# A norm's product and low half on GpSimd instead of VectorE, for fifteen of sixteen pairs of heads

## The chip, the cores and the metric

One core of a Trainium2 chip runs the whole kernel; the other cores do nothing. The metric is the device time of one launch in microseconds (us). The engines are named as in the profile: PE is TensorE (matmuls), PEld its weight loads, DVE is VectorE, ACT is ScalarE, POOL is GpSimd, and SP is the engine whose queue issues most of the DMA transfers. Each engine works through its own instructions in the order in which the program gives them, and waits on semaphores for what the others must have finished.

## The reference

The block computes a layer norm of `x` (2048 rows of 576), an attention with 32 heads of 18, a gated linear unit of width 4608, and joins them:

```
xn = layernorm(x)
q, k, v = heads(xn @ wqkv)                     # 32 heads of 18
p = softmax(q @ k.T * 18 ** -0.5)
s = merge_heads(p @ v) @ wo
h = gelu(xn @ w_gate) * (xn @ w_up)
out = x + s * silu(h @ w_down)
```

The division of the softmax is what this case is about: `p @ v` is summed with unnormalized weights, and each head's sum is multiplied afterwards by the reciprocal of the sum of its weights.

## The kernel before

The products that need precision are done with pairs of 16-bit numbers: a value is split into a high half (the value rounded to 16 bits) and a low half (the value minus the high half), and three matmuls replace one.

Attention goes over 16 pairs of heads. For a pair, the query positions are handled in two halves of 1024 (`qh`), the key positions in 16 tiles. The loop at the end of the program runs over 64 blocks for each pair. A block gives PE one product of keys and queries (`qk2`, L1342), whose exponential ACT takes (L1348, or L1350 and L1351 where the two heads have different scales), and one product for the row maxima of the next pair (`qk1`, L1290), of which DVE takes the maximum (L1293). Each of these two results lives in one double bank of PSUM, so the next block's product waits until ACT, or DVE, has read the last one. The rest of a block's PE time is filled with matmuls of the gated linear unit: gate and up products (L473), down products (L733), and every few blocks a burst of `p @ v` products (L1367), which DVE adds up in a tile `osb` of 128 by 512 (L1375, or L1373 for the first). In the last pair the gate and up products are at an end, and the output products with `wo` (L912) take their place.

POOL carries the gelu of the gated unit: four instructions after ACT has copied the gate product `gs` out of PSUM (L661 to L664), then, when ACT has taken a tanh (L667), two more (L674, L675), and, when ACT has rounded the high half `hhi` (L689), the low half `hlo` (L696). It also makes the low halves of the weights of the next chunks (L342, L343).

When the last burst of a half of a pair is added up, `norm` begins a chain of small steps, each planned some blocks after the one before. Their names in the code are: `a1` and `a2`, two DMA transfers that fetch the sums of weights; `b`, a reciprocal on DVE; `b1` and `b2`, two transfers that spread the reciprocals over the tile `obr`; `c`, the product of `osb` and `obr` (L1421, on DVE); `d`, the high half `onh` (L1425, on ACT); `e`, the low half `onl` as `osb` minus `onh` (L1429, on DVE); `f`, the stores of both halves to DRAM on SP's queue (L1439). There are 30 such chains, two for each of the first 15 pairs. The last pair has another path (`turn`, `divide`, `back`, then the same `d` and `e`).

What order all this has is fixed when the program is written out. `Deferred` holds the steps with a due block and a cost. A step on DVE or ACT is let in when the block has room left on that engine (by a table of costs and rooms), a step on POOL when an estimate of POOL's backlog is at most 1.2. The estimate grows by the cost of each POOL step and shrinks by each block's estimated time. The gelu's steps add to it but are not held back by it. The preparation of weights is a queue of its own, `bg`, that takes what room is left in the same block. So a step that costs DVE nothing leaves its room to `bg`, and a step that costs POOL something holds `bg`'s POOL pieces back.

Of the kernel before, what the change touches and what calls it, by code (L numbers as in the profile page):

```python
# [16 lines left out]
ALU = mybir.AluOpType  # L17
# [64 lines left out]
def on_act(t=0.7):  # L82
    return {"A": t}


def on_dve(t=0.7):
    return {"V": t}


def on_pool(t):  # L90
    return {"G": t}
# [3 lines left out]
def kernel(ctx: ExitStack, tc: tile.TileContext, x, wqkv, wo, w_gate, w_up, w_down, out):  # L95
    nc = tc.nc
# [1260 lines left out]
    def burst(todo, tag):  # L1357

        p, qh, k0, _, _ = todo[0]
        k1 = todo[-1][2]  # L1360
        t = MTile(tag, [P, 512], F32, 1)
        for _, _, kt, pa, pb in todo:
            for b, pt in enumerate((pa, pb)):
                for h in range(2):
                    qd = 64 * b + 32 * h
                    c0 = 38 * kt + 19 * h
                    nc.tensor.matmul(  # L1367
                        t.t[qd:qd + 32, :], VT[p][:, c0:c0 + 32], pt[:, h],
                        start=kt == k0, stop=kt == k1, skip_group_check=True,
                    )  # L1370
        if k0 == 0:
            osum[p, qh] = ap.tile([P, 512], F32, tag="osb", name=f"osb_{p}_{qh}", bufs=2)
            nc.vector.tensor_copy(osum[p, qh], t.t)  # L1373
        else:
            nc.vector.tensor_tensor(osum[p, qh], t.t, osum[p, qh], op=ALU.add)  # L1375
        t.done()
        if k1 == NT - 1:
            norm(p, qh)

    def norm(p, qh):  # L1380
        st = {}
        last = p == NPAIR - 1


        def a():
            st["o"] = osum.pop((p, qh))

        def turn():
            st["b"] = ap.tile([P, 512], F32, tag="obr", name=f"obr_{p}_{qh}", bufs=1)
            nc.vector.transpose(st["b"], st["o"])  # L1390

        def divide():
            b = st["b"].rearrange("p (c i) -> p c i", i=32)
            rc = sm.tile([P, 16], F32, tag="oc", name=f"rc_{p}_{qh}", bufs=2)
            nc.vector.reciprocal(rc, b[:, :, DH])
            nc.vector.tensor_tensor(b, b, rc[:, :, None].to_broadcast([P, 16, 32]), op=ALU.mult)

        def back():
            nc.vector.transpose(st["o"], st["b"])

        def a1():
            st["sd"] = dp.tile([4, 512], F32, tag="sd", name=f"sd_{p}_{qh}", bufs=2)
            nc.sync.dma_start(st["sd"], st["o"][18:128:32, :])

        def a2():
            st["c"] = sm.tile([P, 16], F32, tag="oc", name=f"oc_{p}_{qh}", bufs=2)
            nc.sync.dma_start(st["c"], st["sd"].rearrange("a (b c) -> (a b) c", c=16))

        def b():
            nc.vector.reciprocal(st["c"], st["c"])  # L1410

        def b1():
            st["rd"] = dp.tile([4, 512], F32, tag="rd", name=f"rd_{p}_{qh}", bufs=2)
            nc.sync.dma_start(st["rd"].rearrange("a (b c) -> (a b) c", c=16), st["c"])

        def b2():
            st["b"] = ap.tile([P, 512], F32, tag="obr", name=f"obr_{p}_{qh}", bufs=1)
            nc.sync.dma_start(st["b"], st["rd"][:, None, :].to_broadcast([4, 32, 512]))

        def c():  # L1420
            nc.vector.tensor_tensor(st["o"], st["o"], st["b"], op=ALU.mult)  # L1421

        def d():
            st["h"] = wp.tile([P, 512], F16, tag="evh", name=f"onh_{p}_{qh}", bufs=3)
            nc.scalar.activation(st["h"], st["o"], AF.Copy)  # L1425

        def e():
            st["l"] = wp.tile([P, 512], F16, tag="evl", name=f"onl_{p}_{qh}", bufs=3)
            nc.vector.tensor_tensor(st["l"], st["o"], st["h"], op=ALU.subtract)  # L1429

        def f():
            for qb in range(2):
                cols = slice(1024 * qh + 512 * qb, 1024 * qh + 512 * qb + 512)
                for h in range(2):
                    r = DH * (2 * p + h)
                    qd = 64 * qb + 32 * h
                    for key, rows in (("h", oh_rows), ("l", ol_rows)):
                        for r1, i, n in rows(r, DH):
                            nc.sync.dma_start(OHL[r1:r1 + n, cols], st[key][qd + i:qd + i + n, :])  # L1439
            obdone[qh] += 1  # L1440

        def g():
            last_o[qh] = (st["h"], st["l"])

        def chained(*steps):

            (dt, fn, cost), rest = steps[0], steps[1:]

            def run():
                fn()  # L1450
                if rest:
                    chained(*rest)

            defer.at(defer.now + dt, run, cost)

        a()
        if last:
            final_norm.extend([turn, divide, back, d, e, g])
        else:
            dma = ((1, a1, None), (3, a2, None), (3, b, None), (1, b1, None), (2, b2, None))  # L1460
            chained(*dma, (4, c, on_dve()), (1, d, on_act()), (1, e, on_dve()), (1, f, None))

    ctx.enter_context(tc.manual_schedule())
    filler[0] = unit_v(preps[0])
# [160 lines left out]
    for p in range(NPAIR):  # L1625
# [3 lines left out]
        for i in range(4 * NT):  # L1629
# [24 lines left out]
            if gs.left == 0 and gs.pair is None and not gs.closed and not plan:  # L1654
# [3 lines left out]
                d = dn is not None or (  # L1658
                    len(dnq) > 1 and not (more and 57 < i < 61) and held < 5 and (u is None or not u.wide)
                )  # L1660
# [33 lines left out]
            else:  # L1694
# [4 lines left out]
                if step is None:  # L1699
                    d = dn is not None or len(dnq) > 1 and not 58 <= i <= 60 and held < 6  # L1700
                else:
                    d = step[0]
# [103 lines left out]
```

## Time and profile before

| | |
|---|---|
| median of 3 runs | 2588.85 us (2588.57 to 2589.61) |
| the profiled execution's own time | 2589.88 us |
| its span, first to last instruction | 2588.1 us |
| mean granted PE clock | 0.995 |

The profile lists for each engine its busy time, for groups of equal instructions the busy time, the mean of one, and the idle time of their engine just ahead of them with what ended it. A wait of PE is what costs time here if it isn't covered; a wait of the other engines is often only the sign that they had nothing to do.

### The profile page before, as it was taken

The numbers are of one execution on the slowest core, as the hardware profiler recorded it, in microseconds if no ns is written. First come the engines' busy times: TensorE is split into PE (matmuls) and PEld (weight loads), VectorE is DVE, ScalarE is ACT, GpSimd is POOL, SyncE is SP. The second block draws the span as 40 slices with busy tenths as digits, with TensorE's granted clock in tenths as the row PEclk, the third lists the DMA queues.
The fourth block names the chain that finished last, engine by engine and source line by source line (L and its number), as shares of the span: only waits on it lengthen the run. The fifth ranks groups of instructions, "written<-read, shape, count | busy, mean of one in ns | idle before, by whom it ended". The sixth has DMA issues, their size and how long they took to land.

```text
span 2588.1 us, 60831 instructions
## 1 busy us (share of the span) xinstructions
PE 2503.7 (97%) x25800; PEld 1317.9 (51%) x25800; DVE 1898.9 (73%) x2594; ACT 1661.0 (64%) x2081; POOL 1537.7 (59%) x1564
## 2 busy tenths in 40 slices
PE   6889999999999999999999999999999999999998
PEld 6564545455545545455444444455545444454555
DVE  7587778777777778777777777777777777777644
ACT  5225665666777666767666666767666666766664
POOL 4247663586537553758667575848576676757513
PEclk9999999999999999999999999999999999999999
DMA  4431021201120112102010110101111111110124
GB/s 144 129 104 24 12 58 55 63 18 44 39 86 19 32 32 65 44 24 56 9 50 16 35 52 17 50 15 38 29 34 29 38 29 38 26 32 8 41 63 138
DMA packets 134300, 118.68 MB, mean 46 GB/s; under 512 B 60176, under 2 KB 113064, under 8 KB 134028
## 3 DMA queue, kind: packets, MB, share of 16 engines
q1 hardware_dynamic: 128892, 105.23, 14.9%
q0 software_dynamic: 2432, 6.54, 0.7%
q8 instruction: 201, 3.29, 0.5%
q10 hardware_dynamic: 2704, 3.03, 0.4%
q14 instruction: 71, 0.58, 0.1%
HBM read 84.89 MB, written 29.61 MB: 44 GB/s over the span
## 4 chain that ended last, share of the span: by engine, by line
PE 83%; DVE 6%; ACT 4%; POOL 3%; issue 2%; DMA 1%; ACTq 0%; SPq 0%; DVEq 0%; POOLq 0%
PE mb_t L473 16%; PE ma_t L473 15%; PE md_t L733 15%; PE md_t L1367 10%; PE s L1342 8%; PE s L1290 8%; PE ma_t L1367 6%; DVE PM L1293 2%; ACT P L1348 1%; PE md_t L912 1%; DVE osb L1375 1%; PE mb_t L1367 1%; PE mc_t L492 1%; PE mb_t L912 1%; PE pv_t L492 1%
## 5 line engine op out<-in xcount | busy, mean ns | idle before, releaser
L1293 DVE TENSOR_REDUCE PM<-s 128x2 f32<-128x1024 f32 x1024 | 1251.1, 1224 | 340.4 <-PE s L1290 330.9
L1348 ACT ACTIVATE P<-s,etab 128x1024 f32<-128x1024 f32 x896 | 995.6, 1112 | 605.7 <-PE s L1342 591.4
L473 PE MATMUL ma_t<-XHT,whi_c 64*128 64x512 f16 x1440 | 541.3, 376 | 4.0 <-ACT gs L638 2.4
L473 PE MATMUL mb_t<-XHT,whi_c 64*128 64x512 f16 x1440 | 541.0, 376 | 2.9 <-DVE touch L441 1.2
L473 PE MATMUL ma_t<-XHT,wlo_c 64*128 64x512 f16 x1296 | 486.7, 376 | 0.0
L473 PE MATMUL mb_t<-XHT,wlo_c 64*128 64x512 f16 x1152 | 432.5, 375 | 0.0
L473 PE MATMUL ma_t<-XL,whi_c 64*128 64x512 f16 x1152 | 432.5, 375 | 0.0
L473 PE MATMUL mb_t<-XL,whi_c 64*128 64x512 f16 x1152 | 432.3, 375 | 0.0
L1290 PE MATMUL s<-KT,QT 54*128 54x512 f16 x2048 | 399.0, 378 | 16.7 <-DMA QT<-QD 8.2
L1342 PE MATMUL s<-QT,KT 56*128 56x512 f16 x2048 | 405.3, 379 | 8.4 <-ACT P L1348 4.7
L473 PEld LDWEIGHTS <-whi_c 64*128 64x128 f16 x5184 | 274.1, 94 | 236.9 <-issue 18.0
L733 PE MATMUL md_t<-dhi_c,hhi 64*128 64x288 f16 x2304 | 340.9, 283 | 3.5 <-DVE osb L1375 1.5
L733 PE MATMUL md_t<-dhi_c,hlo 64*128 64x288 f16 x2304 | 340.5, 282 | 0.0
L733 PE MATMUL md_t<-dlo_c,hhi 64*128 64x288 f16 x2304 | 340.0, 282 | 0.0
L733 PEld LDWEIGHTS <-hhi 64*128 64x128 f16 x4608 | 245.2, 94 | 138.1 <-issue 17.6
L674 POOL TENSOR_SCALAR tw<-tw 128x512 f32<-128x512 f32 x144 | 91.0, 632 | 364.0 <-ACT tw L667 363.4
L1367 PE MATMUL md_t<-P,VT 128*32 128x512 f32 x2480 | 290.6, 596 | 0.6 <-ACT P L1348 0.5
L696 POOL TENSOR_TENSOR hlo<-gv,hhi 128x512 f16<-128x512 f32 x144 | 167.6, 1164 | 195.1 <-ACT hhi L689 189.0
L1342 PEld LDWEIGHTS <-KT 56*128 56x128 f16 x2048 | 125.2, 94 | 246.8 <-issue 159.3
L661 POOL TENSOR_TENSOR tw<-gs 128x512 f32<-128x512 f32 x144 | 150.6, 1046 | 127.0 <-ACT gs L638 126.7
L753 DVE SCALAR_TENSOR_TENSOR y<-md_t,c_c,y 128x576 f32<-128x576 f32 x272 | 219.2, 806 | 8.3 <-PE md_t L733 8.2
L473 PEld LDWEIGHTS <-wlo_c 64*128 64x128 f16 x2592 | 138.0, 94 | 122.4
(257 smaller groups left out, 4070.2 us busy)
## 6 DMA issues: line engine op xcount, KB each, us to landing
draw_c<-in_B_w_down SPq DMA_DIRECT2D x18, 576.0 KB
raw_c<-in_B_w_gate SPq DMA_DIRECT2D x18, 512.0 KB
raw_c<-in_B_w_up SPq DMA_DIRECT2D x18, 512.0 KB
obr<-rd SPq DMA_DIRECT2D x30, 256.0 KB
KT<-KD SPq DMA_DIRECT2D x32, 224.0 KB
QT<-QD SPq DMA_DIRECT2D x32, 216.0 KB
VS<-vst POOLq DMA_DIRECT2D x16, 304.0 KB, 3.9
VT<-VS SPq DMA_DIRECT2D x16, 304.0 KB
```

Of the source, the lines that this page charges most:

```text
L473: nc.tensor.matmul(o, lw, xx, start=self.stage == 0 and self.k == 0, stop=self.stage == 1 and self.k == self.slots - 1, skip_group_check=True,
L492: nc.tensor.matmul(o, xx(t), ww[:, t, i, :], start=(k == 0), stop=False)
L661: gp.tensor_tensor(st["t"], st["g"], st["g"], op=ALU.mult)
L674: gp.tensor_scalar(st["t"], st["t"], 1.0, 1.0, op0=ALU.mult, op1=ALU.add)
L696: gp.tensor_tensor(hs.lo[:, ft], st["v"], hs.hi[:, ft], op=ALU.subtract)
L733: nc.tensor.matmul(self.t.t[:, hf, 0:288], a[r, ft, sl], b[r, ft, 288 * hf:288 * hf + 288], start=self.stage == 0 and k == 0, stop=self.st ...
L753: nc.vector.scalar_tensor_tensor(yy, y, w.c, yy, op0=ALU.mult, op1=ALU.add)
L1290: nc.tensor.matmul(s1[:, h], QT[p][r, P * qt:P * qt + P], KT[p][r, 512 * kb:512 * kb + 512], start=True, stop=True)
L1293: nc.vector.tensor_reduce(PM[p][:, :, qt, kb:kb + 1], s1, op=ALU.max, axis=AX.X)
L1342: nc.tensor.matmul(s2[:, h], KT[p][r, P * kt:P * kt + P], QT[p][r, 512 * qb:512 * qb + 512], start=True, stop=True)
L1348: nc.scalar.activation(pt, s2, AF.Exp, scale=ETAB[j0])
L1367: nc.tensor.matmul(t.t[qd:qd + 32, :], VT[p][:, c0:c0 + 32], pt[:, h], start=kt == k0, stop=kt == k1, skip_group_check=True,)
```

## The change

Steps `c` and `e` go from DVE to POOL for the first 15 pairs. Their costs in the planner become POOL costs of 1.1 each, and the due distances of `d` and of `f` grow from one block to two. The last pair's `e` stays on DVE.

```diff
         def c():
-            nc.vector.tensor_tensor(st["o"], st["o"], st["b"], op=ALU.mult)
+            nc.gpsimd.tensor_tensor(st["o"], st["o"], st["b"], op=ALU.mult)
...
         def e():
             st["l"] = wp.tile([P, 512], F16, tag="evl", name=f"onl_{p}_{qh}", bufs=3)
-            nc.vector.tensor_tensor(st["l"], st["o"], st["h"], op=ALU.subtract)
+            (nc.vector if last else nc.gpsimd).tensor_tensor(st["l"], st["o"], st["h"], op=ALU.subtract)
...
             dma = ((1, a1, None), (3, a2, None), (3, b, None), (1, b1, None), (2, b2, None))
-            chained(*dma, (4, c, on_dve()), (1, d, on_act()), (1, e, on_dve()), (1, f, None))
+            chained(*dma, (4, c, on_pool(1.1)), (2, d, on_act()), (1, e, on_pool(1.1)), (2, f, None))
```

Two places show how the instructions stand (pairs and halves are counted from 0). The first is in pair 6, where the chain of the second half of pair 5 (its sum is `osb_1_14475`) reaches `c` and `e`. On DVE, before:

```order
L1375 TENSOR_TENSOR osb_0_15468<-md_t,osb_0_15468 128x512
L1293 TENSOR_REDUCE PM_14859<-s_7_22_15899 128x2
L1421 TENSOR_TENSOR osb_1_14475<-osb_1_14475,obr_1_15787 128x512
L441 COPY touch<-md_t 1x2
L1293 TENSOR_REDUCE PM_14859<-s_7_23_15939 128x2
L753 SCALAR_TENSOR_TENSOR y<-md_t,c_c_13853,y 128x576
```

On DVE with the change, at the same place:

```order
L1375 TENSOR_TENSOR osb_0_15461<-md_t,osb_0_15461 128x512
L1293 TENSOR_REDUCE PM_14859<-s_7_22_15897 128x2
L253 TENSOR_REDUCE m_c_15700<-draw_c_15528 128x1
L441 COPY touch<-md_t 1x2
L1293 TENSOR_REDUCE PM_14859<-s_7_23_15938 128x2
L753 SCALAR_TENSOR_TENSOR y<-md_t,c_c_13891,y 128x576
```

`c` is gone, and a maximum over a chunk's weights (L253, from `bg`) stands where it stood, ahead of the small copy L441 for which PE waits. On POOL at the same place, before:

```order
L675 TENSOR_TENSOR gv_3_0_15664<-gv_3_0_15664,tw_3_0_15698 128x512
L696 TENSOR_TENSOR hlo_3_15847<-gv_3_0_15664,hhi_3_15846 128x512
L661 TENSOR_TENSOR tw_3_1_15904<-gs_3_1_15864 128x512
L662 TENSOR_SCALAR tw_3_1_15904<-tw_3_1_15904 128x512
L663 TENSOR_TENSOR tw_3_1_15904<-tw_3_1_15904,gs_3_1_15864 128x512
L664 TENSOR_TENSOR gv_3_1_15876<-gv_3_1_15876,gs_3_1_15864 128x512
L674 TENSOR_SCALAR tw_3_1_15904<-tw_3_1_15904 128x512
L675 TENSOR_TENSOR gv_3_1_15876<-gv_3_1_15876,tw_3_1_15904 128x512
```

On POOL with the change:

```order
L675 TENSOR_TENSOR gv_3_0_15664<-gv_3_0_15664,tw_3_0_15695 128x512
L696 TENSOR_TENSOR hlo_3_15845<-gv_3_0_15664,hhi_3_15844 128x512
L1421 TENSOR_TENSOR osb_1_14475<-osb_1_14475,obr_1_15785 128x512
L661 TENSOR_TENSOR tw_3_1_15902<-gs_3_1_15862 128x512
L662 TENSOR_SCALAR tw_3_1_15902<-tw_3_1_15902 128x512
L663 TENSOR_TENSOR tw_3_1_15902<-tw_3_1_15902,gs_3_1_15862 128x512
L664 TENSOR_TENSOR gv_3_1_15874<-gv_3_1_15874,gs_3_1_15862 128x512
L1429 TENSOR_TENSOR onl_1_16026<-osb_1_14475,onh_1_15991 128x512
L674 TENSOR_SCALAR tw_3_1_15902<-tw_3_1_15902 128x512
L675 TENSOR_TENSOR gv_3_1_15874<-gv_3_1_15874,tw_3_1_15902 128x512
```

`c` now stands ahead of the gelu's first four steps, and `e` between them and L674. In the whole program the instruction behind `c` or `e` on POOL is L674 in 26 of 60 cases, L661 in 13, L696 in 10, and a weight's L342 in 6.

The second place is in pair 2, where the second half of pair 1 (`osb_1_6027`) is normed while the weights of a chunk are split. On ACT, before:

```order
L1348 ACTIVATE P_0_8_7424<-s_2_0_8_7421,etab_375 128x1024
L1348 ACTIVATE P_1_8_7455<-s_2_1_8_7452,etab_375 128x1024
L1425 ACTIVATE onh_1_7461<-osb_1_6027 128x512
L1348 ACTIVATE P_0_9_7482<-s_2_0_9_7479,etab_375 128x1024
L667 ACTIVATE tw_3_0_7431<-tw_3_0_7431 128x512
```

On ACT with the change:

```order
L1348 ACTIVATE P_0_8_7424<-s_2_0_8_7421,etab_375 128x1024
L1348 ACTIVATE P_1_8_7455<-s_2_1_8_7452,etab_375 128x1024
L1348 ACTIVATE P_0_9_7480<-s_2_0_9_7477,etab_375 128x1024
L1425 ACTIVATE onh_1_7486<-osb_1_6027 128x512
L1348 ACTIVATE P_1_9_7503<-s_2_1_9_7500,etab_375 128x1024
L667 ACTIVATE tw_3_0_7431<-tw_3_0_7431 128x512
```

`d` (L1425) stands one exponential later. On POOL there, before:

```order
L664 TENSOR_TENSOR gv_3_0_7401<-gv_3_0_7401,gs_3_0_7389 128x512
L342 TENSOR_SCALAR draw_c_6191<-draw_c_6191,s_c_6927 128x576
L343 TENSOR_TENSOR dlo_c_7404<-draw_c_6191,dhi_c_7403 128x576
L674 TENSOR_SCALAR tw_3_0_7431<-tw_3_0_7431 128x512
L675 TENSOR_TENSOR gv_3_0_7401<-gv_3_0_7401,tw_3_0_7431 128x512
```

On POOL there, with the change:

```order
L664 TENSOR_TENSOR gv_3_0_7401<-gv_3_0_7401,gs_3_0_7389 128x512
L1429 TENSOR_TENSOR onl_1_7510<-osb_1_6027,onh_1_7486 128x512
L342 TENSOR_SCALAR draw_c_6191<-draw_c_6191,s_c_6927 128x576
L343 TENSOR_TENSOR dlo_c_7404<-draw_c_6191,dhi_c_7403 128x576
L674 TENSOR_SCALAR tw_3_0_7431<-tw_3_0_7431 128x512
L675 TENSOR_TENSOR gv_3_0_7401<-gv_3_0_7401,tw_3_0_7431 128x512
```

`e` has come between L664 and the weights' L342, and it waits for `d`. PE has the same instructions as before, and the same order but for three stretches: some 39 blocks in pairs 2 and 3, 24 blocks in pair 9, and parts of the last pair.

## The prediction

> **What bounds the kernel now.** I read the page first: the busy times and the chain that ended last.
>
> ```profile
> span 2588.1 us, 60831 instructions
> PE 2503.7 (97%) x25800; PEld 1317.9 (51%) x25800; DVE 1898.9 (73%) x2594; ACT 1661.0 (64%) x2081; POOL 1537.7 (59%) x1564
> ...
> PE 83%; DVE 6%; ACT 4%; POOL 3%; issue 2%; DMA 1%; ACTq 0%; SPq 0%; DVEq 0%; POOLq 0%
> ```
>
> PE is busy for 97% of the span and holds 83% of the chain. A busy PE is an upper view (ends of matmuls are modelled), but it says where to look: what DVE loses or POOL gains counts only where PE waits for it. All 30 chains run between 340 and 2480 us, so the second view is the windows, cut there (busy us and instructions of PE, PEld, DVE, ACT, POOL; then granted clock, DMA share, GB/s):
>
> ```profile
> 340.00:2480.00 2140.00, 2110.32 (x21767) 1070.03 (x21763) 1610.62 (x2148) 1446.93 (x1788) 1336.59 (x1326) 1.00 0.14 37
> ```
>
> PE idles 2140.0 - 2110.3 = 29.7 us in that stage. DVE idles 529 us and POOL 803 us. The third view is the waits of PE in the same window (total us, times, longest):
>
> ```profile
> PE ma_t L1367 <- ACT gs L638: 4.3, 9, 1.0
> PE s L1342 <- ACT P L1348: 4.0, 5, 1.6
> PE s L1290 <- DVE PM L1293: 3.5, 6, 1.5
> PE ma_t L473 <- DVE osb L1375: 2.6, 5, 1.0
> PE ma_t L1367 <- DVE evl L524: 1.7, 4, 1.0
> PE md_t L1312 <- DVE osb L1375: 1.6, 2, 0.8
> PE md_t L1312 <- DVE rmc L1306: 1.3, 2, 0.8
> ```
>
> No row names the two moved lines, L1421 and L1429, and POOL is not in them. DVE's five rows here make 10.7 us, ACT's two 8.3. The whole stage offers some 11 us on DVE's side, and ACT's side is already as thin. The fourth view is the groups of instructions in that window (busy us, mean ns, then idle time ahead and what ended it):
>
> ```profile
> L1348 ACT ACTIVATE P<-s,etab 128x1024 f32<-128x1024 f32 x795 | 884.3, 1112 | 543.5 <-PE s L1342 531.1 <-PE s L1290 7.9 <-ACT rms L1314 1.1
> L663 POOL TENSOR_TENSOR tw<-tw,gs 128x512 f32<-128x512 f32 x132 | 168.0, 1273 | 11.1
> L696 POOL TENSOR_TENSOR hlo<-gv,hhi 128x512 f16<-128x512 f32 x133 | 154.9, 1165 | 180.7 <-ACT hhi L689 178.3 <-PE ma_t L473 2.2
> L674 POOL TENSOR_SCALAR tw<-tw 128x512 f32<-128x512 f32 x132 | 83.6, 633 | 342.6 <-ACT tw L667 342.1
> L689 ACT ACTIVATE hhi<-gv 128x512 f16<-128x512 f32 x133 | 82.6, 622 | 6.0 <-POOL gv L675 6.0
> L1421 DVE TENSOR_TENSOR osb<-osb,obr 128x512 f32<-128x512 f32 x30 | 25.8, 860 | 0.6 <-DMA obr<-rd 0.6
> L1429 DVE TENSOR_TENSOR onl<-osb,onh 128x512 f16<-128x512 f32 x30 | 24.1, 802 | 0.1
> L253 DVE TENSOR_REDUCE m_c<-draw_c 128x1 f32<-128x576 f32 x32 | 23.3, 742 | 0.0
> ```
>
> **What the change removes.** DVE loses 25.8 + 24.1 = 49.9 us, 3% of its work in the stage. What that is worth is read where PE waited just behind one of these instructions. One such place, on DVE:
>
> ```profile
> 1143.34 1.22 DVE L1293 TENSOR_REDUCE PM<-s 128x2 f32<-128x1024 f32 x1
> 1144.47 1.11 DVE L1421 TENSOR_TENSOR osb<-osb,obr 128x512 f32<-128x512 f32 x1
> 1145.50 0.14 DVE L441 COPY touch<-md_t 1x2 f32<-1x2 f32 x1
> ```
>
> PE's next instruction there:
>
> ```profile
> 1145.69 0.30 PE L733 MATMUL md_t<-dhi_c,hhi 64*128 64x288 f16 x2 [0.46 <-DVE touch L441]
> ```
>
> The copy L441 had to stand behind `c`, and PE waited 0.46 us for it. I went back from every wait of PE for DVE to see whether `c` or `e` stood in the unbroken run of DVE work ahead of it. There are six such places; these are the first and the last:
>
> ```profile
> 438.51 0.39 PE L1290 MATMUL s<-KT,QT 54*128 54x512 f16 x2 [0.44 <-DVE PM L1293]
> ...
> 1753.04 0.39 PE L1290 MATMUL s<-KT,QT 54*128 54x512 f16 x2 [0.31 <-DVE touch L441]
> ```
>
> At some 0.35 us each (0.46, 0.44 and 0.31 are in the rows above) the six hold 2.1 us. Nor is all of it won: the planner gives the freed room away. At the place shown the changed order has L253 where `c` was, 0.74 us instead of 1.11, so the copy comes only 0.37 us earlier. Bounds of the gain: 0, if other work fills every place, and 10.7 us, if all the DVE waits shown went. I take **1.0 us**, nearer the six places than to anything else.
>
> **What it adds.** POOL gets 30 products and 30 differences. The same shapes stand in its rows: a product of two f32 tiles, L663, 1273 ns; a difference written as f16, L696, 1165 ns. That is 30 x (1.273 + 1.165) = 73.1 us, and POOL's work in the stage goes from 1336.6 to 1409.7 of 2140, 66%. It fits the idle time: 342.6 us ahead of L674 and 180.7 ahead of L696, waiting for ACT, just where the changed order puts 36 of the 60.
>
> Here a rule speaks against the change. The Trainium skill, GPSIMD Engine Reference, section 4.1 Engine selection, puts two-input elementwise work on VectorE, because GpSimd is about twice as slow at it. The rows give 1273 against 860 for the product, a factor of 1.5, and DVE's rows include its own stretched ones. By the rule's factor an estimate of POOL's gain in work would be 2 x 49.9 = 99.8 us instead of 73.1, and its share 67%; either way POOL is far from full, so the rule decides only if POOL's lateness reaches ACT.
>
> That is the next price. A POOL instruction that comes 1.2 us late makes ACT wait if ACT had less to spare, and then the exponential behind it. At the place shown:
>
> ```profile
> 1149.94 0.80 POOL L674 TENSOR_SCALAR tw<-tw 128x512 f32<-128x512 f32 x1 [4.91 <-ACT tw L667]
> 1150.82 1.27 POOL L675 TENSOR_TENSOR gv<-gv,tw 128x512 f32<-128x512 f32 x1
> ```
>
> and ACT's use of that result:
>
> ```profile
> 1153.73 0.62 ACT L689 ACTIVATE hhi<-gv 128x512 f16<-128x512 f32 x1
> ```
>
> POOL idled 4.91 us ahead of L674, where `e` will stand, and ACT took L675's result 1153.73 - 1152.09 = 1.64 us after its end: `e`'s 1.17 us are covered twice. In 26 places L674 is next behind `c` or `e`. ACT waits for L675 for 6.0 us in the stage now, so a few places have no margin. And a late exponential is covered again: it waits for PE for 543.5/795 = 0.68 us on the mean. Bounds: 0, and 26 x 1.2 = 31 us if no place had cover. I take two places at 0.5 us, **1.0 us** lost, near the end that these rows show. Without the cover each place costs up to 1.2 us.
>
> **Two new waits on POOL.** `e` waits for `d` with the gelu and the weights' splits queued behind it. In pair 2 `d` moves one exponential back:
>
> ```profile
> 552.42 1.71 POOL L664 TENSOR_TENSOR gv<-gv,gs 128x512 f32<-128x512 f32 x1
> 554.12 1.74 POOL L342 TENSOR_SCALAR draw_c<-draw_c,s_c 128x576 f32<-128x576 f32 x1
> ```
>
> ```profile
> 554.13 1.11 ACT L1348 ACTIVATE P<-s,etab 128x1024 f32<-128x1024 f32 x1 [0.32 <-PE s L1342]
> ```
>
> `d` would then end at 554.13 + 1.11 + 0.62 = 555.86, `e` at about 557.1, and L342 would start 3 us late, with L674 behind it. The weights' halves and `hlo` are not due at once, and in the changed order the `hhi` that follows stands further back too; I count nothing beyond the 1.0 above. `c` waits for the last DMA, `obr`. Only in one chain did DVE wait for it; POOL's next gelu there, and DVE's `c`:
>
> ```profile
> 1805.54 1.04 POOL L661 TENSOR_TENSOR tw<-gs 128x512 f32<-128x512 f32 x1 [1.39 <-ACT gs L638]
> ```
>
> ```profile
> 1806.98 0.84 DVE L1421 TENSOR_TENSOR osb<-osb,obr 128x512 f32<-128x512 f32 x1 [0.60 <-DMA obr<-rd]
> ```
>
> On POOL `c` stands ahead of that L661 and still ends no earlier than 1806.98 + 1.27 = 1808.25, so L661 starts 2.7 us late. Bounds 0 and 2.7; tanh is not the next thing ACT does, so I take **0.3 us**.
>
> **What it moves.** `f` issues the same transfers on SP's queue, planned up to two blocks later in the chain. It matters once, when the output products read what the first half of pair 14 stored:
>
> ```profile
> 2433.58 1.80 SPq L848 DMA_DIRECT2D ohl<-OHL  x1
> ```
>
> ```profile
> 2447.77 0.28 PE L912 MATMUL ma_t<-whi_wo,ohl 64*128 64x288 f16 x1
> ```
>
> The load was issued 14.2 us ahead of its first use; two blocks of at most 2588.1/1024 = 2.5 us (16 pairs of 64 blocks) leave most of that. I count nothing; if the load were late, PE would lose those blocks' 5 us once. Last, the planner writes three stretches of PE's work in another order, each about a window of 100 us. What the order of a stretch is worth is seen from the spread between such windows (two of twenty from 400 us, and their sum):
>
> ```profile
> 1000.00:1100.00 100.00, 96.77 (x892) 44.34 (x890) 76.58 (x96) 67.64 (x78) 51.61 (x53) 1.00 0.22 62
> 2000.00:2100.00 100.00, 99.73 (x1052) 49.84 (x1046) 74.77 (x100) 63.33 (x73) 62.07 (x61) 1.00 0.11 29
> sum 2000.00, PE 1972.72 PEld 997.06 DVE 1517.68 ACT 1352.13 POOL 1266.78; mean PE 98.64 PEld 49.85 DVE 75.88 ACT 67.61 POOL 63.34
> ```
>
> PE's idle time goes from 0.3 to 3.2 us a window, 1.4 on the mean: half that spread, 1.5 us, for each of three stretches, either sign. I take 0, with 4.5 us as its bound.
>
> **Sum.** Span 2588.1 - 1.0 + 1.0 + 0.3 = 2588.4 us. The profiled execution took 1.8 us more than its span, so 2590.2; and it was 1.0 us above the median of the runs. That gives **2589.1 us**, 0.01% above before: nothing that a measurement tells from no change, for which I take 0.2%, 5.2 us. Its own range is 2584 to 2594.
>
> **Rivals.**
>
> *Slower: POOL's lateness reaches PE through ACT.* POOL, 1.5 times as slow as DVE by the rows above, delays L675, ACT's `hhi` waits, and the exponentials behind it come late; PE's L1342 waits, as it does for 4.0 us now. For it: ACT already waits 6.0 us for L675, and 26 places are exposed. Against: POOL's idle time stands at these very places. If half of the 26 lose their whole 1.2 us and 0.68 of it is covered, 13 x 0.5 = 7 us: 2589.1 - 1.0 + 7 = 2595. It decides from the point where ACT has under half a microsecond to spare behind L675 in most chains. The Trainium skill's rule on elementwise work, named above, points this way.
>
> *Faster: DVE's relief goes further than the six places.* Maxima start earlier all along, and over half of the 10.7 us goes without loss elsewhere: 2588.85 - 6 = 2583. For it: the longest DVE wait, 1.5 us, stands behind a maximum L1293. Against: 3% less work, and the room is given to `bg`.
>
> *It doesn't do what it says:* the freed room on DVE is filled everywhere and POOL's work is fully covered. Then 2588.85 us; inside the forecast.
>
> **How the numbers follow.** Forecast with the third rival 0.69, slower 0.18, faster 0.13. The slower case's 2595 and the reordering's bound on top of the faster one (2583 - 1) set the range of 2582 to 2596. Faster by over 0.2% 0.13, within it 0.69, slower 0.18.
>
> **What would show it.** DVE's busy time falls by some 50 us less its stretched remainder, POOL's rises by about 73; L1421 and L1429 on POOL take 1.27 and 1.17 us. PE's idle time in the stage stays near 30 us; ACT's wait for L675 stays below 10 us, and a value over 20 with more waits of L1342 for ACT means the slower rival. PE's waits for DVE under 6 us mean the faster one. A wait of PE for `ohl`, or for weights split late, would prove the nothings above wrong.

## The result, and the profile after

| | before | changed |
|---|---|---|
| median of 20 runs each, on one chip | 2589.09 us (2587.52 to 2590.85) | 2593.9 us (2590.83 to 2595.31) |
| ratio | | 1.0019, 95% interval 1.0013 to 1.0025 |
| span of the profiled execution | 2588.1 us | 2592.4 us |

The change costs 4.8 us, 0.19%. The forecast was 2589.1 within 2582 to 2596 and "no change" by a bound of 0.2%: the time lies in the range and just inside the bound, on its slow side. The interval excludes 1, so there is a loss to explain.

The page of the changed kernel, with busy time by engine and the chain that ended last:

```profile
span 2592.4 us, 60873 instructions
PE 2504.7 (97%) x25800; PEld 1323.1 (51%) x25800; DVE 1859.6 (72%) x2535; ACT 1661.0 (64%) x2081; POOL 1596.6 (62%) x1624
...
PE 81%; DVE 7%; POOL 3%; ACT 3%; DMA 2%; issue 2%; SPq 1%; ACTq 0%; POOLq 0%; DVEq 0%
```

The work moved as it should: DVE has 39.3 us less (1898.9 before), POOL 58.9 us more (1537.7). In the chain, PE's share fell from 83% to 81% and that of DMA rose from 1% to 2%. This is the first hint, since the change adds no transfer. The stage of the chains, cut 4 us later because the changed kernel runs that much late (busy us by PE, PEld, DVE, ACT, POOL):

```profile
340.00:2484.00 2144.00, 2109.65 (x21703) 1073.72 (x21698) 1567.61 (x2084) 1444.82 (x1785) 1390.44 (x1382) 1.00 0.14 37
```

PE idles 2144.0 - 2109.65 = 34.4 us there, 29.7 before: 4.7 us more. PE's waits in the same window (total us, times, longest) name where:

```profile
PE s L1290 <- DVE PM L1293: 5.0, 9, 1.5
PE s L1342 <- DMA QT<-md: 4.4, 2, 4.1
PE ma_t L1367 <- ACT gs L638: 4.0, 8, 1.2
PE ma_t L912 <- DVE ob L956: 2.4, 2, 1.8
PE ma_t L473 <- DVE osb L1375: 2.0, 5, 0.8
PE s L1342 <- ACT P L1348: 1.1, 5, 0.3
```

Two rows were not among those shown of before. PE waits 4.1 us in one place for `QT<-md`, the transfer that puts the row maxima into two rows of the queries' tile. It also waits for `ob` (L956), the step with which DVE reads an output product out of PSUM. One row got better: the wait for the exponential L1348, 4.0 before, is 1.1. The groups of moved and neighbouring instructions, and ACT's wait for POOL's gelu:

```profile
L1421 POOL TENSOR_TENSOR osb<-osb,obr 128x512 f32<-128x512 f32 x28 | 35.6, 1272 | 10.7 <-DVE osb L1375 5.6 <-DVE touch L441 5.1
...
L1429 POOL TENSOR_TENSOR onl<-osb,onh 128x512 f16<-128x512 f32 x29 | 33.5, 1156 | 44.2 <-ACT onh L1425 44.2
L674 POOL TENSOR_SCALAR tw<-tw 128x512 f32<-128x512 f32 x132 | 81.5, 618 | 296.6 <-ACT tw L667 296.2
L689 ACT ACTIVATE hhi<-gv 128x512 f16<-128x512 f32 x133 | 82.7, 622 | 6.1 <-POOL gv L675 4.1 <-DMA QT<-md 2.0
```

POOL's new steps take 1272 and 1156 ns each (two of the 30 products and one of the differences lie outside this window), and the 44.2 us that POOL waits ahead of `e` for `d` are idle time of an engine with time to spare. ACT waits for L675 4.1 us instead of 6.0, but for L663, the other result of POOL that it needs, 4.3 us instead of 2.3. So POOL made ACT no later on the whole (8.4 us against 8.3), and no earlier.

To see where the 4.3 us arise, I took the start of every block's L1342 (there are 1024 blocks) in both traces and subtracted. The lateness of three kernels against the kernel before, in us. The two at the right come from the experiments below: "held" lets SP's loads wait for the row maxima's transfer, and "0 to 13" makes the change for the first 14 pairs only.

| block | changed | changed, held | 0 to 13, held |
|---|---|---|---|
| 180 | -1.6 | -1.5 | -1.2 |
| 192 | -2.6 | -2.5 | -2.1 |
| 224 | +0.4 | +0.6 | +1.3 |
| 321 | +1.2 | +0.1 | +0.8 |
| 575 | -1.3 | -2.3 | -1.7 |
| 577 | **+4.7** | -2.3 | -1.7 |
| 731 | +1.5 | -6.2 | -5.5 |
| 900 | +1.4 | -5.7 | -5.1 |
| 976 | **+8.2** | +1.2 | -5.0 |
| 1023 | +4.4 | -2.6 | -6.2 |

The first column gains, and gives it back in two places: 6.0 us at the start of pair 9 (blocks 575 to 577) and 3.0 net in the last pair (900 to 1023). Where PE's work is in another order (blocks 183 to 219, 599 to 620 and 957 to 1012), a block holds other work than before. So 180 and 224 can be compared, but a value between them, such as that of 192, is neither a gain nor a loss.

**Pair 9.** The queues before, around 1540 us (SP's first, then ACT's, and `e` on DVE):

```profile
1527.20 0.26 SPq L1439 DMA_DIRECT2D OHL<-onh  x1
1540.74 0.26 SPq L1439 DMA_DIRECT2D OHL<-onl  x1
...
1543.94 1.41 SPq L229 DMA_DIRECT2D raw_c<-in_B_w_gate  x1
```

```profile
1542.92 0.46 ACTq L1316 DMA_DIRECT2D md<-rms  x1
...
1545.09 0.54 ACTq L1320 DMA_DIRECT2D QT<-md  x2
```

```profile
1540.03 0.68 DVE L1429 TENSOR_TENSOR onl<-osb,onh 128x512 f16<-128x512 f32 x1
```

SP stood behind the store of `onl` from 1527.5 to 1540.7, because `e` ran only at 1540.03. So the weights' loads (L229) went out at 1543.94, behind the maxima's first transfer `md<-rms`. Its second, which needs the first, followed after 2.2 us (1542.92 to 1545.09). The same with the change, SP, ACT and POOL:

```profile
1521.40 0.26 SPq L1439 DMA_DIRECT2D OHL<-onl  x1
...
1540.52 0.41 SPq L229 DMA_DIRECT2D raw_c<-in_B_w_gate  x1
```

```profile
1541.63 0.48 ACTq L1316 DMA_DIRECT2D md<-rms  x1
...
1547.80 0.54 ACTq L1320 DMA_DIRECT2D QT<-md  x2
```

```profile
1520.21 1.16 POOL L1429 TENSOR_TENSOR onl<-osb,onh 128x512 f16<-128x512 f32 x1
...
1539.33 1.16 POOL L343 TENSOR_TENSOR wlo_c<-raw_c,whi_c 128x512 f16<-128x512 f32 x1
```

```profile
1552.13 0.54 PE L1342 MATMUL s<-QT,KT 56*128 56x512 f16 x2 [4.13 <-DMA QT<-md]
```

`e` is done at 1521.4, 19 us sooner, and the stores are gone. SP now waits only for a free buffer, which POOL's L343 gives at 1540.49: the load starts at 1540.52, 1.1 us *ahead* of `md<-rms`. From there to the second transfer it takes 6.2 us instead of 2.2, and pair 9 cannot start without it.

The wait is 4.13 us, but the blocks lose 6.0. Most of the rest is PE's own pace behind the wait. Two stretches of 4 us of the changed kernel, before and behind it (columns as above; the granted clock is the third figure from the end):

```profile
1544.00:1548.00 4.00, 4.00 (x48) 2.36 (x42) 3.19 (x4) 0.86 (x1) 3.92 (x4) 1.00 0.46 151
1552.10:1556.10 4.00, 3.97 (x27) 2.84 (x29) 2.04 (x2) 1.11 (x1) 2.97 (x2) 0.60 0.02 4
```

Behind the wait the clock is 0.60 on the mean, which loses 0.4 x 4.0 = 1.6 us; the products L473 start 0.43 us apart there and 0.22 us apart before the wait.

**The last pair.** PE's waits of L912 in 2435 to 2592, before and changed:

```profile
PE md_t L912 <- DVE touch L441: 2.7, 2, 2.5
PE mb_t L912 <- DVE touch L441: 2.2, 3, 1.5
```

```profile
PE ma_t L912 <- DVE ob L956: 3.0, 3, 1.8
PE md_t L912 <- DVE touch L441: 1.1, 2, 0.8
```

The planner ends the gate and up products one block earlier and starts the output products one block earlier; new waits for `ob` take the place of others, and the balance is a loss.

**Where the gain comes from.** At block 724 the changed kernel wins 1.8 us in one place, and 1.1 us more at block 731, where ACT had waited 1.46 us for L675. POOL, ACT and PE at block 724, before:

```profile
1887.19 1.56 POOL L342 TENSOR_SCALAR raw_c<-raw_c,s_c 128x512 f32<-128x512 f32 x1
1888.83 1.15 POOL L343 TENSOR_TENSOR wlo_c<-raw_c,whi_c 128x512 f16<-128x512 f32 x1
...
1891.95 1.26 POOL L675 TENSOR_TENSOR gv<-gv,tw 128x512 f32<-128x512 f32 x1
```

```profile
1893.25 0.63 ACT L689 ACTIVATE hhi<-gv 128x512 f16<-128x512 f32 x1 [2.36 <-POOL gv L675]
```

```profile
1894.93 0.39 PE L1342 MATMUL s<-QT,KT 56*128 56x512 f16 x2 [1.62 <-ACT P L1348]
```

and changed:

```profile
1892.28 1.15 POOL L1429 TENSOR_TENSOR onl<-osb,onh 128x512 f16<-128x512 f32 x1
1893.41 0.61 POOL L674 TENSOR_SCALAR tw<-tw 128x512 f32<-128x512 f32 x1
1894.11 1.27 POOL L675 TENSOR_TENSOR gv<-gv,tw 128x512 f32<-128x512 f32 x1
...
1897.26 1.56 POOL L342 TENSOR_SCALAR raw_c<-raw_c,s_c 128x512 f32<-128x512 f32 x1
```

```profile
1895.41 0.63 ACT L689 ACTIVATE hhi<-gv 128x512 f16<-128x512 f32 x1 [0.21 <-POOL gv L675]
```

Before, 4 us of a weight's split stood between the gelu's two parts and ACT waited 2.36 us, PE 1.62 behind it. With the change `e` stands there, its 1.1 counts in the planner's estimate of POOL's backlog, and the split is held back behind L675. `e` is slower on POOL than on DVE and still makes POOL's result earlier for ACT, since it keeps out something longer. The place at 1538 us (block 572, where 1.8 us are won) shows the same pair of waits before (1.99 and 1.61 us) and neither after.

### The profile page after: what moved, and what is told of

Its sections match the earlier page's. It is cut to its first block, busy times and chain, and to the rows that moved or that the text cites. A ratio compares the mean times of both kernels' runs of the same rounds, so it can differ in the third digit from the quotient of the medians.

```text
span 2592.4 us, 60873 instructions
## 1 busy us (share of the span) xinstructions
PE 2504.7 (97%) x25800; PEld 1323.1 (51%) x25800; DVE 1859.6 (72%) x2535; ACT 1661.0 (64%) x2081; POOL 1596.6 (62%) x1624
## 4 chain that ended last, share of the span: by engine, by line
PE 81%; DVE 7%; POOL 3%; ACT 3%; DMA 2%; issue 2%; SPq 1%; ACTq 0%; POOLq 0%; DVEq 0%
PE mb_t L473 16%; PE ma_t L473 15%; PE md_t L733 15%; PE md_t L1367 9%; PE s L1342 8%; PE s L1290 8%; PE ma_t L1367 6%; DVE PM L1293 2%; ACT P L1348 1%; PE mb_t L912 1%; POOL raw_c L342 1%; DVE osb L1375 1%; PE md_t L912 1%; DMA QT<-QD 1%; PE pv_t L492 1%
## 5 line engine op out<-in xcount | busy, mean ns | idle before, releaser
L1293 DVE TENSOR_REDUCE PM<-s 128x2 f32<-128x1024 f32 x1024 | 1251.4, 1224 | 354.1 <-PE s L1290 346.9
L1348 ACT ACTIVATE P<-s,etab 128x1024 f32<-128x1024 f32 x896 | 995.0, 1112 | 609.7 <-PE s L1342 594.5
L473 PE MATMUL ma_t<-XHT,whi_c 64*128 64x512 f16 x1440 | 542.5, 377 | 3.2 <-ACT gs L638 2.4
L473 PE MATMUL mb_t<-XHT,whi_c 64*128 64x512 f16 x1440 | 542.3, 377 | 2.2 <-ACT gv L649 1.1
L473 PE MATMUL ma_t<-XHT,wlo_c 64*128 64x512 f16 x1296 | 487.7, 376 | 0.0
L473 PE MATMUL mb_t<-XHT,wlo_c 64*128 64x512 f16 x1152 | 433.6, 376 | 0.0
L473 PE MATMUL ma_t<-XL,whi_c 64*128 64x512 f16 x1152 | 433.6, 376 | 0.0
L473 PE MATMUL mb_t<-XL,whi_c 64*128 64x512 f16 x1152 | 433.5, 376 | 0.0
L1342 PE MATMUL s<-QT,KT 56*128 56x512 f16 x2048 | 405.9, 380 | 9.2 <-DMA QT<-md 4.4
L473 PEld LDWEIGHTS <-whi_c 64*128 64x128 f16 x5184 | 275.6, 94 | 233.1 <-issue 15.2
L1367 PE MATMUL md_t<-P,VT 128*32 128x512 f32 x2504 | 293.6, 596 | 1.7 <-DVE osb L1375 0.8
L674 POOL TENSOR_SCALAR tw<-tw 128x512 f32<-128x512 f32 x144 | 89.0, 618 | 316.8 <-ACT tw L667 316.3
L696 POOL TENSOR_TENSOR hlo<-gv,hhi 128x512 f16<-128x512 f32 x144 | 166.8, 1159 | 182.7 <-ACT hhi L689 176.9
L1342 PEld LDWEIGHTS <-KT 56*128 56x128 f16 x2048 | 125.9, 94 | 248.6 <-issue 157.1
L661 POOL TENSOR_TENSOR tw<-gs 128x512 f32<-128x512 f32 x144 | 150.1, 1043 | 84.1 <-ACT gs L638 83.6
L473 PEld LDWEIGHTS <-wlo_c 64*128 64x128 f16 x2592 | 138.6, 94 | 121.2 <-issue 0.3
```

The costliest lines, as they stand in the source:

```text
L473: nc.tensor.matmul(o, lw, xx, start=self.stage == 0 and self.k == 0, stop=self.stage == 1 and self.k == self.slots - 1, skip_group_check=True,
L661: gp.tensor_tensor(st["t"], st["g"], st["g"], op=ALU.mult)
L674: gp.tensor_scalar(st["t"], st["t"], 1.0, 1.0, op0=ALU.mult, op1=ALU.add)
L696: gp.tensor_tensor(hs.lo[:, ft], st["v"], hs.hi[:, ft], op=ALU.subtract)
L1293: nc.vector.tensor_reduce(PM[p][:, :, qt, kb:kb + 1], s1, op=ALU.max, axis=AX.X)
L1342: nc.tensor.matmul(s2[:, h], KT[p][r, P * kt:P * kt + P], QT[p][r, 512 * qb:512 * qb + 512], start=True, stop=True)
```

## The experiments

In all of them only the norm's steps, the planner's numbers for them, or SP's queue are touched. Times are medians, each beside the kernel before on the same chip.

**1 to 4: which half of the change costs?** The change is two things: the engines of `c` and `e`, and the planner's costs and distances for them. Theory: the new order. Rival: the engines. The engines alone:

```diff
-            nc.vector.tensor_tensor(st["o"], st["o"], st["b"], op=ALU.mult)
+            nc.gpsimd.tensor_tensor(st["o"], st["o"], st["b"], op=ALU.mult)
...
-            nc.vector.tensor_tensor(st["l"], st["o"], st["h"], op=ALU.subtract)
+            (nc.vector if last else nc.gpsimd).tensor_tensor(st["l"], st["o"], st["h"], op=ALU.subtract)
```

> c and e run on POOL, but the planner is told the old costs and distances, so every queue has the order of the kernel before and only the engine of 60 instructions differs. If the planner's new order cost the 4.8 us (order theory), this stays within 2 us of before, near 2588, since DVE is relieved and nothing is moved. If POOL's lateness costs it (engine theory), this is 3 to 6 us slower than before, and PE's waits for ACT grow by as much.

Measured: 2600.18 against 2588.89, ratio 1.0039 (1.0026 to 1.0053): 11.3 us slower, more than the whole change. The plan alone:

```diff
-            chained(*dma, (4, c, on_dve()), (1, d, on_act()), (1, e, on_dve()), (1, f, None))
+            chained(*dma, (4, c, on_pool(1.1)), (2, d, on_act()), (1, e, on_pool(1.1)), (2, f, None))
```

> c and e stay on DVE, but the planner is told the new costs and distances, so PE and SP have the order of the changed kernel. Order theory: 3 to 7 us slower than before, with the tail of pair 15 (some +3.4 us between the blocks 959 and 1008) and the long wait for the maxima's DMA at the start of pair 9 (4.3 us) in it. Engine theory: within 2 us of before.

Measured: 2608.34 against 2588.89, 1.0072 (1.006 to 1.0085): 19.5 us slower. Only `c` moved:

```diff
-            nc.vector.tensor_tensor(st["o"], st["o"], st["b"], op=ALU.mult)
+            nc.gpsimd.tensor_tensor(st["o"], st["o"], st["b"], op=ALU.mult)
...
-            chained(*dma, (4, c, on_dve()), (1, d, on_act()), (1, e, on_dve()), (1, f, None))
+            chained(*dma, (4, c, on_pool(1.1)), (2, d, on_act()), (1, e, on_dve()), (1, f, None))
```

> Only c goes to POOL, with its new cost and distance; e and f as before. PE's order comes out as in the changed kernel. Order theory: 3 to 6 us slower than before. Engine theory: half of the loss, some 2.4 us. If the wait at pair 9 hangs on e being early (SP's queue is freed sooner and loads collide with the maxima's transfer), this run has no such wait.

Measured: 2594.07 against 2588.89, 1.0021 (1.0012 to 1.003), as the whole change. Only `e` moved:

```diff
-            nc.vector.tensor_tensor(st["l"], st["o"], st["h"], op=ALU.subtract)
+            (nc.vector if last else nc.gpsimd).tensor_tensor(st["l"], st["o"], st["h"], op=ALU.subtract)
...
-            chained(*dma, (4, c, on_dve()), (1, d, on_act()), (1, e, on_dve()), (1, f, None))
+            chained(*dma, (4, c, on_dve()), (1, d, on_act()), (1, e, on_pool(1.1)), (2, f, None))
```

> Only e goes to POOL, with its new cost and f's distance; c as before. PE's order comes out as in the kernel before. Order theory: within 2 us of before, unless the wait at pair 9 is there, which adds 4 us. Engine theory: half of the loss, some 2.4 us.

Measured: 2597.4 against 2588.89, 1.0041 (1.0028 to 1.0053).

The halves do not add (11.3 and 19.5 against 4.8), so neither theory holds as it was put; only `c` alone came out as one of them, the order, had it. The traces say why the halves are worse than the whole. The engines alone, ACT's wait for POOL, then PE's waits in the stage:

```profile
ACT hhi L689 <- POOL gv L675: 10.2, 7, 3.2
```

```profile
PE s L1342 <- ACT P L1348: 5.6, 5, 2.4
PE s L1342 <- DMA QT<-md: 5.5, 2, 3.0
```

With `c` and `e` on POOL but not in the planner's backlog, nothing is held back for them: POOL is late for ACT by 10.2 us in all, where the changed kernel has 4.1, and PE waits for the exponential. That is the slower rival of the prediction, and what keeps it away is the planner's part of the change: around the blocks 572 and 724, where the changed kernel wins 1.8 us each, this run loses 2.5 and 0.8. The plan alone, PE's waits:

```profile
PE s L1342 <- DMA QT<-md: 4.4, 1, 4.4
...
PE md_t L733 <- DVE y L753: 3.8, 8, 0.7
PE md_t L733 <- DVE osb L1375: 3.1, 3, 2.1
```

Here the planner gives away room on DVE that `c` and `e` still use, and PE waits for DVE. What all four have in common is a wait for `QT<-md` of 4.1 to 5.9 us in total, where before had 0.4. It is not always at pair 9: `c` alone and the plan alone have it there (3.9 and 4.4 us), the engines alone at the pairs 6 and 9 (3.0 and 2.5), `e` alone mostly at pair 3 (3.3, and 0.8 at pair 9). The run with `c` alone was expected to have none at pair 9 if the wait hung on `e` being early, and that was a miss. `e` stands on DVE there and is early all the same:

```profile
1523.32 0.68 DVE L1429 TENSOR_TENSOR onl<-osb,onh 128x512 f16<-128x512 f32 x1
```

That is 17 us earlier than before. With `e` alone on POOL it runs at 1541.09, about as late as before. So what brings `e` and its stores forward at pair 9 is the new place that the planner gives to `c`, and with it to `d` and `e`, and not the engine of `e`. This made the collision on the queues the next theory.

**5 and 6: hold SP's loads back.** Two rows of the queries' tile are read back to SBUF by a tiny transfer on SP's queue right after the maxima were written there. SP cannot pass it before they have landed, so the loads behind it cannot start earlier. In the changed kernel, and in the kernel before as a control:

```diff
+            if p > 0:
+                hold = dp.tile([2, 64], F16, tag="hold", name=f"hold{p}", bufs=2)
+                nc.sync.dma_start(hold, QT[p][118:120, S - 64:S])
```

> The changed kernel, with one transfer of 256 bytes more for each pair: SP reads two rows of the next pair's query tile that the maxima's transfer (QT<-md) has just written, so SP's queue sends no weights until that has landed. PE's order is unchanged. If the 4.3 us wait of PE at the start of pair 9 comes from the weights' transfers going out ahead of the maxima's, it is gone and the time falls to about 2590. If the transfer is slow for another reason, the time stays at 2594 and the wait stays.

Measured: 2588.8 against 2588.47, 1.0003 (0.9994 to 1.0012), 5.1 us below the changed kernel's 2593.9, which comes from other runs. The queues at pair 9 in this kernel, SP and ACT:

```profile
1543.82 0.22 SPq L1326 DMA_DIRECT2D hold<-QT  x1
1544.80 1.39 SPq L229 DMA_DIRECT2D raw_c<-in_B_w_gate  x1
```

```profile
1539.84 0.46 ACTq L1316 DMA_DIRECT2D md<-rms  x1
...
1542.01 0.53 ACTq L1320 DMA_DIRECT2D QT<-md  x2
```

The loads start behind the maxima's transfers, and these are 2.2 us apart again. The wait of PE for `QT<-md` is gone.

> The kernel before with the same extra transfer, as a control: PE waits there for QT<-md for 0.4 us in all, so nothing is to be won. Expected within 1 us of before, 2588 to 2590; a gain of 3 us or more would say that the guard helps by something else than that collision.

Measured: 2589.73 against 2588.47, 1.0004 (0.9995 to 1.0013). The same read gains nothing in the kernel before, which has no collision to lose. So the gain with the change is not a gift of the read itself.

**7: the last pair's order.** The change for pairs 0 to 13 only; PE's order in the last pair is then that of before.

```diff
+        moved = p < 14
...
-            nc.gpsimd.tensor_tensor(st["o"], st["o"], st["b"], op=ALU.mult)
+            (nc.gpsimd if moved else nc.vector).tensor_tensor(st["o"], st["o"], st["b"], op=ALU.mult)
...
-            (nc.vector if last else nc.gpsimd).tensor_tensor(st["l"], st["o"], st["h"], op=ALU.subtract)
+            (nc.gpsimd if moved else nc.vector).tensor_tensor(st["l"], st["o"], st["h"], op=ALU.subtract)
...
-            chained(*dma, (4, c, on_pool(1.1)), (2, d, on_act()), (1, e, on_pool(1.1)), (2, f, None))
+            if moved:
+                chained(*dma, (4, c, on_pool(1.1)), (2, d, on_act()), (1, e, on_pool(1.1)), (2, f, None))
+            else:
+                chained(*dma, (4, c, on_dve()), (1, d, on_act()), (1, e, on_dve()), (1, f, None))
```

> The change for the first 14 pairs alone; pair 14 keeps the old chain, and the last pair's PE order comes out as in the kernel before. If the order of the last pair costs the +3.4 us between the blocks 959 and 1008, the time falls from 2593.9 to about 2590.5 and the block times of the last pair run parallel to those of before. If that loss is in the engines, it stays at 2593 or more.

Measured: 2590.03 against 2588.47, 1.0004 (0.9995 to 1.0012), 3.9 us below the whole change. The waits of L912 for `ob` are gone, and the collision at pair 9 is still there (3.9 us).

**8 and 9: both, and a smaller hold.** First the two together:

> Both together. If the two losses are separate and the rest of the change is a gain of some 3 us (block times of the changed kernel, -2.7 us by block 208 and -1.8 and -2.9 us at the blocks 572 and 724 to 731, against +2 to +3 us elsewhere), the time is 2586 to 2587, 2 to 3 us below before. If they share a cause, it is 2590.

Measured: 2585.8 against 2588.47, 0.999 (0.9981 to 0.9998). The two add. But the read made a new wait in the last pair, where SP's load of `ohl` had to stand behind it (this kernel; 2.1 us in run 5 and 1.4 in run 6):

```profile
PE ma_t L912 <- DMA ohl<-OHL: 1.5, 1, 1.5
```

So the read is left out for the last pair:

```diff
-            if p > 0:
+            if 0 < p < NPAIR - 1:
```

> As the kernel with the change for 14 pairs and the guard, without the guard in front of the last pair, where PE waited 1.5 us for the output products' load (ohl) in the guarded kernels and not in the others. If the guard holds SP's queue there, the wait goes and the time falls from 2585.8 to about 2584.5. If the wait has another cause, it stays and so does the time.

Measured: 2582.7 against 2588.86, 0.9977 (0.9968 to 0.9986): 6.2 us faster than before and the best of all. It won 3 us where 1.5 were expected. In run 8 the granted clock behind that wait is 0.59 from 2443 to 2447 us, which loses 1.6 us more, and its blocks lose 3.2 us there (960 to 962); in run 6 the wait of 1.4 us has a clock of 1.00 behind it, and the blocks lose 1.6. PE's longest waits in this kernel, from 340 us to its end (L1345 and L1370 are the lines L1342 and L1367 of before, moved by three):

```profile
PE s L1290 <- DVE PM L1293: 5.2, 10, 1.5
PE ma_t L1370 <- ACT gs L638: 2.8, 7, 0.4
...
PE s L1345 <- ACT P L1351: 1.6, 7, 0.3
```

No transfer is among its waits any more. DVE's maxima are now the largest row. Of its lead over the kernel before in the block table, 1.7 us come at the blocks 994 to 997, where the kernel before has a stretch of slow clock at 2512 us and this one has none.

**10: the hold with the engines alone.** If the collision is all that the hold takes away, it should win no more here than its waits held.

> c and e on POOL with the planner's old costs, and the guard (not in front of the last pair). The collision theory takes away the 5.5 us for which PE waits for QT<-md there: 2600.2 falls to 2594 to 2595. What is left over the kernel before, some 6 us, is then POOL's lateness reaching ACT (2.6 us waits of PE's L1342 for ACT), because the planner didn't count the two steps. If the 11 us were POOL's lateness alone, the guard changes nothing: 2599 to 2601.

Measured: 2591.57 against 2588.86, 1.0009 (1.0 to 1.0018). That is 8.6 us less than run 1, against 5.5 us of waits for `QT<-md` there. The sign is as expected, and the size was a miss. The blocks of run 1 show the excess: the two starts of pairs cost 5.8 us (pair 6) and 2.7 us (pair 9), 8.5 together, because the clock behind the first wait is 0.54 from 1104.5 to 1112 us, which loses 3.4 us more. What is left, 2.7 us above before, is the late POOL, as far as the waits show: PE's total for the exponential (L1348 there is L1351) is 6.3 us from 340 us to the end, 4.4 before. All of PE's waits for ACT come to 16.5 us against 11.7, those for DVE to 19.4 against 21.7.

**11 and 12: whose gain is it?** Run 9 has the change and a hold, so both were tried apart: the hold of run 9 on the kernel before, and on the whole change.

> The control for the fastest kernel: the kernel before with the two-row read on SP behind each pair's row maxima, for the pairs 1 to 14 alone, nothing else changed. The read at all pairs cost it 1.3 us (2589.7 against 2588.5), of which one wait of PE for a transfer of the last pair's ohl was 1.4 us. Theory (the gain belongs to the norm's work on GpSimd, and the read only takes away a collision that the kernel before does not have): that wait goes, and the kernel is at the time of the kernel before within 1 us, 2588 to 2590. Rival (the read itself is the gain, whatever the norm's engine): it gains as the change for the pairs 0 to 13 does with it, some 6 us, about 2583.

Measured: 2588.73 against 2588.97, ratio 1.0 (0.9991 to 1.0009). The hold alone is worth nothing.

> The changed kernel with the two-row read for the pairs 1 to 14 alone. With the read at all pairs but the first it took 2588.8 against 2588.5 before, with a wait of 2.1 us of PE for the last pair's ohl. Theory (three separate terms: the collision, this wait, the last pair's order): the wait goes and the order's 3.9 us stay, as 2582.7 + 3.9 = 2586.6 and 2588.8 - 2.1 = 2586.7 both say: 2586 to 2587.5, 2 us below the kernel before. Rival (the terms are not separate, and the last pair's loss went with the read): about 2583, as the change for the pairs 0 to 13 with the same read. A kernel at 2588.8 or above would say that the wait for ohl only hid another.

Measured: 2585.98 against 2588.97, 0.9992 (0.9983 to 1.0001), as the first theory said (2586 to 2587.5, missed by 0.02). The collision, the wait for `ohl` and the last pair's order are separate terms. This is the kernel of the middle column above.

## Why the prediction was right, and where it was not

The time was within the range by luck: terms that were counted as nothing and a term that was counted too small have opposite signs. From the table of blocks: relief of -5.7 by block 900 once the loads are held, +6.0 at pair 9, +3.1 in the last pair (900 to 1023 in the middle column), and +1.3 at block 320. There the same collision holds ACT up at the start of pair 5: a load of 304 KB (`VT<-VS`) goes out 1.15 us ahead of `md<-rms`, `QT<-md` follows after 4.6 us instead of 2.2, and PE's L1367 waits for ACT; with the loads held this loss is gone. Together +4.7; the changed kernel shows +4.4 in the last block.

- **"What it moves", `f` and SP's queue: counted as nothing, and wrong.** The prediction said that `f` "issues the same transfers" and asked only whether a store could be late for `ohl`. That wait did not come in the changed kernel. The stores came *earlier*, and a store that stands in SP's queue also holds back everything behind it. With the obstacle gone, weights' loads overtook the row maxima's transfer: +6.0 us at pair 9 and +1.3 at pair 5. Held, the kernel takes 5.1 us less with the new wait for `ohl` (run 5) and 7.9 us less without it (run 12). The queue was asked who comes late, not who comes early.
- **The three reordered stretches: taken as 0, bound 4.5 either way.** The first (blocks 183 to 219) costs 2.0 us, from -1.6 at block 180 to +0.4 at 224. It is the order that costs it: the plan alone, with the engines of before, loses 2.4 us between these blocks, and the engines alone, with the order of before, win 0.3. The second (599 to 620) comes to -0.2; the collision of pair 9 lies ahead of it. The last pair's costs 3 to 4 us by itself (3.9 in run 7; +3.1 in the blocks). Together they make some 5 us, all on the slow side and just over the bound.
- **DVE's relief: 1.0 us, within 0 to 10.7.** Mis-sized and mostly misplaced. With the collision and the last pair's order out of the way the change wins 6.2 us (run 9), but the waits that went are not DVE's: from 340 us to the end PE's waits for DVE go from 21.7 to 22.7 us (L1293 from 3.5 to 5.2) and those for ACT from 11.7 to 7.0. So run 9 has the faster rival's number, 2583, by another mechanism. The bound was read too low as well: the list of before goes on with smaller waits for DVE of 4.4 us in all, so it should have been 15.1. That the planner gives the freed room away was right: the plan alone, which does so while `c` and `e` still run on DVE, is the slowest of all.
- **POOL's lateness through ACT: +1.0 us, the wait for L675 below 10 us.** The size was harmless, and the sign for L675 was wrong. It fell from 6.0 to 4.1 because the planner, which now sees a POOL cost, holds the splits back. The places at 1538 and 1893 us show it. The wait for L663, which had no term, rose by as much, from 2.3 to 4.3. The engines-alone run, without that cost, gives 10.2 us and a slower kernel, so the rival was real and lay one line of the diff away.
- **`c` waiting for `obr`, `e` for `d`: 0.3 and 0.** POOL waits 44.2 us for `d`, and the waits above name no one who waits for `c` or `e`. The runs measured neither alone.
- **What would show it.** POOL's new lines were forecast at 1.27 and 1.17 us and took 1.272 and 1.156. DVE's busy time fell by 39.3 (50 forecast) and POOL's rose by 58.9 (73 forecast); part of the latter is that other POOL groups got shorter (L674 83.6 to 81.5). PE's idle time in the stage came to 34.4 us, where some 30 were forecast. The sign given for the "nothings" was a wait of PE for `ohl` or for weights split late, and neither came. The sign that came, a wait for `QT<-md`, stood in the list of before with 0.4 us, and the prediction did not name it.

What stays open: why the output products are worse off one block earlier beyond the 3.0 us for `ob` (the profiles of both kernels have one stretch of slow clock in the last pair, so that is not it), and why some of PE's waits are followed by a slow clock and others of the same length are not. Run 9 is the fastest kernel here; whether a hold at fewer pairs does as well was not tried.

## What to carry to other kernels

A step that finishes earlier is a change too: list what stands behind it in its in-order queue, and what small transfer with a deadline those loads will now run ahead of; a tiny dependent read on that queue tests it, and may be the remedy. When work moves to another engine, move its cost in the planner with it, and test the two halves apart: here each half alone was worse than both. A small sum of small terms can hide larger ones of both signs, so compare block by block before calling a change neutral. A long wait of PE can cost more than its length: read the granted clock behind it.

## What the runs showed of the hardware

- A 16 KB transfer on ACT's queue and the one that depends on it were 2.2 us apart when issued ahead of the weights' loads, and 6.2 us when issued 1.1 us behind their start on SP's queue; held back, they were 2.2 us apart again. Another queue gave it no path of its own. This fits a rule of the Trainium skill, DMA: Bandwidth & Descriptors, section "Issuing engines are not separate DMA queues": transfers started by different engines run on the same 16 DMA engines and interleave.
- PE's granted clock falls to a half behind some of its waits. In the 14 traces, from 340 us to 30 us before the end, there are 16 such stretches, 3.4 us each and one of 6.8, and every one lies at the end of a wait of PE of 1.5 us or more, or within 2 us of it. All 6 waits over 2.6 us have one, of the 40 between 1.5 and 2.6 us only 10: the same wait of 2.50 us for L441 in the last pair has one in the kernel before and none in run 9. A stretch of 3.4 us at a half costs 1.7 us.
- The product `c` on DVE has no single price. All 30 in the kernel before (ns, minimum, median, maximum):

```profile
L1421 DVE TENSOR_TENSOR osb<-osb,obr x30: 669/714/1558, 343.8 to 2470.9; 128x512 f32<-128x512 f32 x30
```

  The six that took 1107 ns or more had a two-input instruction of POOL (TENSOR_TENSOR) running beside them for 51 to 100% of their time; of the 16 that took 728 ns or less, 13 had one for under a fifth. On POOL it takes 1272 ns: 1.9 times DVE's fastest, but faster than DVE's slowest. The factor of 1.5 in the prediction came from DVE's mean of 860. The Trainium skill's factor of about 2 (GPSIMD Engine Reference, section 4.1 Engine selection) agrees with the fastest ones. It did not decide the time here: the order that the planner wrote did.
